# Loads that wait for earlier loads: each of the first 44 transfers into SBUF starts once another, 600 KB further ahead, has landed

## The chip, the core and the metric

The kernel runs on one NeuronCore of a Trainium2 chip. The core has a matrix engine (TensorE, PE in the tables, with its weight loads as PEld), a vector engine (DVE), a scalar engine (ACT), a general engine (POOL) and a sync engine (SP) that only issues transfers here. Each engine works through its own list of instructions in order, and semaphores hold one engine back until another, or a transfer, is done. Transfers between HBM and SBUF are carried out by 16 DMA engines. The metric is the device time of one execution in microseconds (us); lower is better.

## What is computed

Three layers follow each other, in fp32, on 4 x 576 tokens of width 512 (8 heads of 64):

```python
# 1: attention; a pooled part (means over 4 tokens) plus a local band of |i - j| < 4
out_d = sm_attn(q_d, k_d, v_d)                      # q_d, k_d, v_d: means over groups of 4
scores = np.where(mask, scale * q @ k.T, -1e9)
x = np.repeat(out_d, 4) + softmax(scores) @ v
# 2: gated feed-forward with a depthwise convolution over the tokens
h = np.maximum(x @ w_in, 0.0)                       # 512 -> 1024
x = h * sigmoid(conv3(h, conv_w)) @ w_out           # 1024 -> 512
# 3: low-rank token mixing, then a feed-forward with a residual
u = x + (x.T @ U @ V).T
out = u + np.maximum(u @ w_ch1, 0.0) @ w_ch2        # 512 -> 2048 -> 512
```

The weights of layers 2 and 3 arrive as 64-bit floats, twice the bytes of fp32, and are turned into pairs of fp32 tiles (a high and a low part) on the chip.

## The kernel before

The work is written as one long list of words, `SEQ`. Each word names a step and its indices, and the kernel emits the steps in exactly that order; every engine then executes its own share in that order. Nothing is reordered afterwards.

**Attention** runs over 16 pairs of heads, p = 0 to 15. A pair needs three loads: `lq` (`load_qk`, line 286, 576 KB), `lw` (`load_vw`, line 291, 384 KB) and `lr` (`load_vr`, line 295, 288 KB on 72 partitions). Its steps, with their lines, are: sums over groups of four (L300, DVE), scores (L317 and L324, PE), maxima, shift, exponentials and row sums (L339, L346, L352, L356), pooled scores and their exponentials (L377, L382, L389), sums of four rows of v (`vs`, L401 and L404, mostly POOL), normalisation (L370 and L394, POOL), transposes (L411 and L418, PE) and their copies out of PSUM (`c` L423, `cd` L428, ACT or DVE), the products with v (`V` L438 with 96 small matmuls, `Vd` L446, PE), and `xd` (L454) and `x` (L465), which write the result into the tile X. The step `f` (L279) is a few extra matmuls between them.

**Weights**: `wl` (`w_load`, line 485, 512 KB) loads one raw 128 x 512 tile of 64-bit words. `wd` decodes it in four steps: L495 on ACT, then L497, L499 and L502 on DVE. `wh` (L515, ACT) and `wo` (L518, mostly POOL) make the two fp32 tiles of it. 16 such tiles belong to layer 2, 32 to layer 3. In `SEQ` the loads and decodes of layer 2 stand between the steps of the attention.

**Layer 2** (g L631, acc L685) starts at about 60 us beside the attention; **layer 3** (g L759, acc L777) fills the second half of the run.

**All loads are issued by SP**, one after the other, in the order of `SEQ`: `ident` (64 KB), `maskf` (96 KB), then qk, vw, vr of pairs 0 and 1, qk and vw of pair 2, the convolution weights `craw` (24 KB), the raw tiles 1.0 to 1.2, qk of pair 3, vr of pair 2, qk of pair 4, vr of pair 3, raw tile 1.3, and so on. An issue waits for whatever still uses the buffer that it fills. Beside that there are eight semaphores for transfers, used in turn, so that a transfer also waits for the landing of the one eight before it. The 19 stores of the result come behind all the loads.

Of the kernel before, what the change touches and what calls it, by code (L numbers as in the profile page):

```python
# [9 lines left out]
U32 = mybir.dt.uint32  # L10
# [171 lines left out]
P = 128  # L182
# [5 lines left out]
def mixer_kernel(ctx, tc, consts, qk, vw_, vr_, w1, w2, cw_, u_, v_, out):  # L188
    nc = tc.nc
# [9 lines left out]
    NCH = TB // P  # L199
    XW = TB + 4  # L200
    KPB = 3
    SD = S // 4
    SCALE = D ** -0.5
    NK = cw_.shape[1] // NF
    Z = 2 if w1.dtype == U64 else 1
# [14 lines left out]
    pst = tc.alloc_tile_pool(name="pst", bufs=1, space=PSUM, side="right", reuse_waits="tile")  # L220
    pools = {}


    ident = const.tile([P, P], F32, name="ident")
    identR = pa.tile([P, P], F32R, name="identR")
    maskf = pa.tile([P, 6 * NW], F32, name="maskf")
# [4 lines left out]
    cw = const.tile([P, NK * NF], F32, name="cw")  # L231

    def load_consts():
        nc.sync.dma_start(ident, consts[:, :P])
        nc.sync.dma_start(maskf, consts[:, P:])

    def make_consts():
        nc.vector.tensor_copy(identR, ident)
# [42 lines left out]
    def slot_b(n, name):  # L281
        return (ps0 if n < 1 else pst).tile([P, 512], F32, name=name, tag=f"b{n}")

    def load_qk(p):
        t = (xu if p % 3 == 2 else pa).tile([P, 2, S], F32, name="qk", tag=("qk0", "qk1", "xu3")[p % 3])
        nc.sync.dma_start(t, qk[p])
        st[p]["qk"] = t

    def load_vw(p):
        t = st[p]["vw"] = pa.tile([P, 3, 4, D], F32, name="vw", tag="vw", bufs=3)  # L290
        nc.sync.dma_start(t.rearrange("p t a d -> p (t a d)"), vw_[p])

    def load_vr(p):
        t = st[p]["vr"] = xu.tile([72, 4, 2, 2, D], F32, name="vr", tag=f"xu{4 + p % 2}")
        nc.sync.dma_start(t.rearrange("p t h c d -> p (t h c d)"), vr_[p])

    def sums(p):
        e = st[p]
        t = e["ss"] = pa.tile([P, 2, SD], F32, name="ss", tag="ss", bufs=2)
        nc.vector.tensor_reduce(out=t.rearrange("p z x -> p (z x)"),  # L300
# [71 lines left out]
    def scores_d(p, n):  # L372
        e = st[p]
        t = slot_b(n, "Sd")
        s = e["Sd"] = t[:96, :3 * SD].rearrange("p (j x) -> p j x", j=3)
        for j in range(3):
# [7 lines left out]
    def exps_d(p):  # L384
        e = st[p]
        t = e["Pd"] = pa.tile([96, 3, SD], F32, name="Pd", tag="Pd", bufs=2)
        s = e.pop("Sd")
# [4 lines left out]
    def norm_d(p, eng):  # L392
        e = st[p]
        eng.tensor_tensor(e["Pd"], e["Pd"], e["sm"][:96, 12:].unsqueeze(2).to_broadcast([96, 3, SD]), op=ALU.mult)  # L394

# [45 lines left out]
    def pv_pooled(p):  # L441
        e = st[p]
        pt = e["PTd"].rearrange("p c (j r) -> p c j r", j=3)
        for h in range(2):
            for c in range(2):
                nc.tensor.matmul(e["O"][D * h:D * h + D, 0, 288:288 + SD].rearrange("p (j r) -> p j r", j=3),  # L446
                                 e["vd"][:, h, c], pt[:, c, :, 48 * h:48 * h + 48], start=c == 0, stop=c == 1)

    def copy_od(p, eng):
        e = st[p]  # L450
        t = e["xd"] = pa.tile([P, SD], F32, name="xd", tag="xd", bufs=2)
        src = e["O"][:, 0, 288:288 + SD]
# [21 lines left out]
    def w_home(k):  # L474
        g, i = k
        if g == 1 or NAW2 <= i < NAW2 + N1:
            return wp, f"w{i if g == 1 else i - NAW2}"
        return (pools["wa"], f"wa{i}") if i < NAW2 else (pools["wb"], f"wb{i - NAW2 - N1}")

    def w_load(*k):  # L480
        pool, tag = w_home(k)
        t = pool.tile([P, 512 * Z], U32 if Z == 2 else F32, name="raw", tag=tag)
        raws[k] = t.rearrange("p (n z) -> p n z", z=Z)
        src = (w1, w2)[k[0] - 1][k[1]]
        nc.sync.dma_start(t, src.bitcast(U32) if Z == 2 else src)

    def dec(raw, dst, step):
        if raw.shape[2] == 1:
# [31 lines left out]
    craw = const.tile([P, NK * NF * Z], U32 if Z == 2 else F32, name="craw")  # L520

    def load_conv():
        nc.sync.dma_start(craw, cw_.bitcast(U32) if Z == 2 else cw_)

    def conv_weights(step):
        dec(craw.rearrange("p (n z) -> p n z", z=Z), cw, step)
# [6 lines left out]
    def words(t, n):  # L533
        return (t[:, :n * Z].bitcast(U32) if Z == 2 else t[:, :n]).rearrange("p (n z) -> p n z", z=Z)

    def uv_load(w):
        n = u_.shape[1] if w == 0 else v_.shape[1]
        t = xu.tile([P, 1536], F32, name="uvr", tag=("xu2", "xu1")[w])
        raw = words(t, n)
        if w == 0:  # L540
            uv["t"] = t
            val = t[:, 640:640 + n]
        else:
            val = uv["t"][:, 960:960 + n]
        uv[w] = raw, val
        src = (u_, v_)[w]
        nc.sync.dma_start(raw.rearrange("p n z -> p (n z)"), src.bitcast(U32) if Z == 2 else src)

    def uv_dec(w, step):
        dec(*uv[w], step)  # L550
# [151 lines left out]
    def mix_in(g, c, odd):  # L702
        t = x2[g, c]
        pair, j = divmod(g * NCH + c, KPB * NCH)
        b = 2 * pair + odd
# [26 lines left out]
    def mix_add(pair, j):  # L732
        g, c = divmod(pair * KPB * NCH + j, NCH)
        u = U_[g][:, c]
        nc.vector.tensor_tensor(u, u, mx.pop((pair, j)), op=ALU.add)
# [44 lines left out]
    def flush4(g, c):  # L780
# [8 lines left out]
    DV, GP = nc.vector, nc.gpsimd  # L789
    ACTS = {  # L790
        "k": load_consts, "K": make_consts, "xz": x_pads, "z": clear, "sf": spin_fill, "sp": spin, "f": beat, "wm": warm,
        "lq": load_qk, "lw": load_vw, "lr": load_vr, "qs": sums, "qd": q_blocks, "S": scores, "M": maxima,
        "D": shifted, "E": exps, "R": rowsums, "re": lambda p: eps_add(p, P, 0, 15), "r": lambda p: recip(p, P, 0, 15),
        "n": lambda p: norm(p, GP), "nv": lambda p: norm(p, DV),
# [85 lines left out]
```

## Time and profile before

| | |
|---|---|
| median of 3 runs | 755.89 us (755.01 to 756.33) |
| the profiled execution, its own time | 755.43 us |
| its span, from the first to the last instruction | 753.7 us |
| PE busy, of the span | 733.5 us, 97% |
| DVE, ACT, POOL busy | 399.0, 297.2, 170.3 us |
| moved by the DMA engines | 52.43 MB |

The difference between the profiled execution's own time and its span, 1.7 us, lies around the program and is the same work for any version of it. PE is busy nearly throughout, but not evenly: the page's slices show it at 7 tenths in the first three of its 40 slices (57 us) and at 9 tenths or more from there on. So a reader should look at the first 60 us apart from the rest. Times below are counted from the start of the span.

### The profile page before, as it was taken

Reading aid. Unit: us, or ns where it says so; the run is one execution under the profiler, and the core shown is the slowest. Engines: PE = TensorE matmul, PEld = TensorE weight load, DVE = VectorE, ACT = ScalarE, POOL = GpSimd, SP = SyncE. Lnnn points to the kernel's source line nnn. Section 1 sums busy time; section 2 is a strip of 40 time slices with the busy share of each in tenths; the row PEclk is TensorE's granted clock in tenths of the full one; section 3 lists DMA queues with packets and bytes.
Section 4 is the critical chain, followed back from the end, with each engine's and each line's share of the span. In section 5 each row is a group of like instructions: output and inputs, shape, how many; then the busy total and the mean of one; then the engine's idle time right before and its main releaser. Section 6 shows DMA issues by size and latency. Waiting matters only on the chain.

```text
span 753.7 us, 15425 instructions
## 1 busy us (share of the span) xinstructions
PE 733.5 (97%) x6650; PEld 653.6 (87%) x6650; DVE 399.0 (53%) x647; ACT 297.2 (39%) x668; POOL 170.3 (23%) x161
## 2 busy tenths in 40 slices
PE   7779999999999999999999999999999999999998
PEld 5669888988988889988888989989989989898996
DVE  5798998987567984898997111311121131112112
ACT  4556777465557764766453111211111121111110
POOL 3667664352225542232222000000000000000000
PEclk9558999999999999999999999999999999999999
DMA  9855442411022001370240000100010010001001
GB/s 316 290 175 186 164 156 97 138 58 36 1 62 108 1 0 29 103 289 28 90 191 29 15 0 1 43 0 1 1 43 0 1 43 1 1 0 43 1 1 42
DMA packets 16388, 52.43 MB, mean 70 GB/s; under 512 B 1984, under 2 KB 2496, under 8 KB 16320
## 3 DMA queue, kind: packets, MB, share of 16 engines
q1 hardware_dynamic: 16320, 51.44, 19.9%
q8 instruction: 52, 0.85, 0.5%
q14 instruction: 16, 0.13, 0.1%
HBM read 46.72 MB, written 4.72 MB: 68 GB/s over the span
## 4 chain that ended last, share of the span: by engine, by line
PE 84%; DVE 9%; DMA 3%; ACT 2%; issue 2%; SPq 0%; POOL 0%; DVEq 0%; ACTq 0%
PE g L759 26%; PE acc L777 26%; PE g L631 11%; PE acc L685 10%; PE O L438 2%; DVE wval L499 2%; DMA raw<-in_w_dram 2%; DVE wval L497 1%; PE S L324 1%; DVE wval L502 1%; DMA vr<-in_vr_dram 1%; PE Sd L377 1%; PE O L446 1%; PE ut L743 1%; DVE g L658 1%
## 5 line engine op out<-in xcount | busy, mean ns | idle before, releaser
L759 PE MATMUL g<-uT,w 128*128 128x384 f32 x1152 | 214.8, 338 | 0.6 <-DVE a L768 0.6
L777 PE MATMUL acc<-w,a 128*128 128x512 f32 x864 | 208.6, 392 | 0.0
L759 PEld LDWEIGHTS g<-uT,w 128*128 128x128 f32 x1152 | 201.7, 188 | 7.5 <-DVE a L768 3.5
L768 DVE SCALAR_TENSOR_TENSOR a<-g,a 128x384 fp32r<-128x384 f32 x96 | 53.5, 557 | 264.8 <-ACT a L764 264.7
L777 PEld LDWEIGHTS acc<-w,a 128*128 128x128 f32 x864 | 160.9, 188 | 31.9 <-issue 0.6
L764 ACT ACTIVATE a<-g 128x384 fp32r<-128x384 f32 x96 | 47.1, 491 | 283.4 <-PE acc L777 165.6
L631 PE MATMUL g<-xhl,w 128*128 128x386 f32 (+1 forms) x576 | 115.4, 347 | 1.0 <-DVE ct L669 1.0
L685 PE MATMUL acc<-w,ghl 128*128 128x512 f32 x432 | 108.3, 395 | 0.0
L631 PEld LDWEIGHTS g<-xhl,w 128*128 128x128 f32 x576 | 101.8, 191 | 6.0 <-DVE ct L669 2.3
L685 PEld LDWEIGHTS acc<-w,ghl 128*128 128x128 f32 x432 | 79.6, 188 | 16.0 <-ACT u L692 0.5
L677 POOL TENSOR_TENSOR ghl<-ct,ghl 128x384 fp32r<-128x384 f32 x48 | 50.6, 1056 | 105.7 <-ACT ghl L674 86.1
L658 DVE SCALAR_TENSOR_TENSOR g<-h,cw,g 128x384 f32<-128x384 f32 x96 | 59.1, 619 | 27.2 <-ACT g L653 25.6
L518 POOL TENSOR_TENSOR w<-wval,w 128x512 fp32r<-128x512 f32 x32 | 42.8, 1341 | 58.1 <-ACT w L515 55.5
L499 DVE SCALAR_TENSOR_TENSOR wval<-raw,wval 128x512 uint32<-128x512 uint32 x48 | 43.5, 907 | 1.3
L515 ACT ACTIVATE w<-wval 128x512 fp32r<-128x512 f32 x48 | 29.8, 628 | 35.6 <-DVE wval L502 35.4
L502 DVE SCALAR_TENSOR_TENSOR wval<-raw,wval 128x512 uint32<-128x512 uint32 x48 | 41.6, 878 | 0.8
L438 PEld LDWEIGHTS O<-PT,vw 32*64 32x64 f32 x1536 | 27.9, 149 | 8.4 <-issue 7.3
L438 PE MATMUL O<-PT,vw 32*64 32x24 f32 x1536 | 29.8, 224 | 4.5 <-issue 4.4
L495 ACT ACTIVATE wval<-raw 128x512 f32<-128x512 f32 x48 | 31.3, 665 | 4.4 <-DMA raw<-in_w_dram 2.7
L637 ACT ACTIVATE h<-g 128x386 f32<-128x386 f32 (+1 forms) x48 | 23.6, 491 | 23.9 <-PE g L631 23.5
L662 ACT ACTIVATE g<-g 128x384 f32<-128x384 f32 x48 | 22.7, 473 | 21.1 <-DVE g L658 21.0
L674 ACT ACTIVATE ghl<-ct 128x384 fp32r<-128x384 f32 x48 | 25.1, 522 | 14.8 <-PE acc L685 9.8
(92 smaller groups left out, 647.3 us busy)
## 6 DMA issues: line engine op xcount, KB each, us to landing
raw<-in_w_dram SPq DMA_DIRECT2D x48, 512.0 KB
qk<-in_qk_dram SPq DMA_DIRECT2D x16, 576.0 KB
vw<-in_vw_dram SPq DMA_DIRECT2D x16, 384.0 KB
vr<-in_vr_dram SPq DMA_DIRECT2D x16, 288.0 KB
out_dram<-u SPq DMA_DIRECT2D x17, 256.0 KB
uvr<-in_v_dram SPq DMA_DIRECT2D x1, 576.0 KB
uvr<-in_u_dram SPq DMA_DIRECT2D x1, 320.0 KB
out_dram<-u SPq DMA_DIRECT2D x2, 128.0 KB
```

Of the source, the lines that this page charges most:

```text
L438: nc.tensor.matmul(o[D * h:D * h + D, jh, c:c + NQ], e["vw"][32 * s:32 * s + 32, t, a], e["PT"][32 * s:32 * s + 32, t, 32 * a:32 * a + NQ] ...
L499: nc.vector.scalar_tensor_tensor(out=d, in0=lo, scalar=29, in1=d, op0=ALU.logical_shift_right, op1=ALU.bitwise_or)
L502: nc.vector.scalar_tensor_tensor(out=d, in0=hi, scalar=0x80000000, in1=d, op0=ALU.bitwise_and, op1=ALU.bitwise_or)
L518: eng.tensor_tensor(W[k][:, 1], vals.pop(k), W[k][:, 0].bitcast(F32), op=ALU.subtract)
L631: nc.tensor.matmul(gp[n][:, :wd], w[:, a, cc], xhl[g, cc][:, b, :wd], start=cc == 0 and i == 0, stop=cc == NCC - 1 and i == 2)
L658: nc.vector.scalar_tensor_tensor(out=o, in0=inner(g, hts[n], k), scalar=cw[:, k * NF + f:k * NF + f + 1], in1=o, op0=ALU.mult, op1=ALU.add)
L677: eng.tensor_tensor(ghl[n][:, 1], cts.pop(n), ghl[n][:, 0].bitcast(F32), op=ALU.subtract)
L685: nc.tensor.matmul(acc[g][c], t[:, a, c * P:(c + 1) * P], w[:, b], start=f == 0 and i == 0, stop=f == NF - 1 and i == 2)
L759: nc.tensor.matmul(gp["3", m][:, :TB], w[:, a, cc], uT[g, cc][:, b, :TB], start=cc == 0 and i == 0, stop=cc == NCC - 1 and i == 2)
L764: nc.scalar.activation(out=t[:, 0], in_=gp["3", m][:, :TB], func=AF.Relu)
L768: nc.vector.scalar_tensor_tensor(out=t[:, 1], in0=gp.pop(("3", m))[:, :TB], scalar=0.0, in1=t[:, 0].bitcast(F32), op0=ALU.max, op1=ALU.sub ...
L777: nc.tensor.matmul(acc2[g][c], t[:, a, c * P:(c + 1) * P], w[:, b], start=f == 0 and i == 0, stop=f == NF2 - 1 and i == 2)
```

## The change

The five kinds of loads, the constants and the convolution weights go through a new function `load`, which is given the tile, the source and the size in KB. For the first 44 calls it looks back through the transfers already issued, adds up their sizes from the latest one on until the sum is 600 KB or more, and makes the new transfer wait for the landing of the one ahead of those. The order of the issues, the sizes, and all that the other engines do stay as they are.

```diff
+    WAY, NLIM = 600, 44
...
+    queue = []
+
+    def load(t, src, n):
+
+        i = nc.sync.dma_start(t, src)
+        if len(queue) < NLIM:
+            k, later = len(queue) - 1, 0
+            while k >= 0 and later < WAY:
+                later += queue[k][1]
+                k -= 1
+            if k >= 0:
+                tc.add_manual_dep(getattr(i, "ins", i), queue[k][0].name, mybir.DependencyInfo(
+                    mybir.DependencyClass.Sync, mybir.DependencyReason.DATA), reason="transfers under way")
+            queue.append((getattr(i, "ins", i), n))
...
-        nc.sync.dma_start(ident, consts[:, :P])
-        nc.sync.dma_start(maskf, consts[:, P:])
+        load(ident, consts[:, :P], 64)
+        load(maskf, consts[:, P:], 96)
...
-        nc.sync.dma_start(t, qk[p])
+        load(t, qk[p], 576)
...
-        nc.sync.dma_start(t.rearrange("p t a d -> p (t a d)"), vw_[p])
+        load(t.rearrange("p t a d -> p (t a d)"), vw_[p], 384)
...
-        nc.sync.dma_start(t.rearrange("p t h c d -> p (t h c d)"), vr_[p])
+        load(t.rearrange("p t h c d -> p (t h c d)"), vr_[p], 288)
...
-        nc.sync.dma_start(t, src.bitcast(U32) if Z == 2 else src)
+        load(t, src.bitcast(U32) if Z == 2 else src, 512)
```

No instruction moves on any engine; only the waits of SP's issues differ. On SP, at the start of the program, the kernel before has these waits from the sixth issue on (DMAHW0 to DMAHW7 are the eight semaphores of transfers: the first transfer, ident, counts on DMAHW0, maskf on DMAHW1, the first qk on DMAHW2 and so on in turn; DVE, PE and Pool stand for a buffer that the engine still uses):

```order
L286 DMA qk<-in_qk_dram 128x1152
L291 DMA vw<-in_vw_dram 128x768
L295 DMA vr<-in_vr_dram 72x1024
L286 DMA qk<-in_qk_dram 128x1152 [waits DMAHW0_49]
L291 DMA vw<-in_vw_dram 128x768 [waits DMAHW1_49]
L523 DMA craw<-in_cw_dram 128x48 [waits DMAHW2_49]
L485 DMA raw<-in_w_dram 128x1024 [waits DMAHW3_49]
L485 DMA raw<-in_w_dram 128x1024 [waits DMAHW4_49]
L485 DMA raw<-in_w_dram 128x1024 [waits DMAHW5_49]
```

The changed kernel has, at the same place on SP (line 228 is inside `load`):

```order
L228 DMA qk<-in_qk_dram 128x1152 [waits DMAHW2_49]
L228 DMA vw<-in_vw_dram 128x768 [waits DMAHW3_49]
L228 DMA vr<-in_vr_dram 72x1024 [waits DMAHW4_49]
L228 DMA qk<-in_qk_dram 128x1152 [waits DMAHW5_49]
L228 DMA vw<-in_vw_dram 128x768 [waits DMAHW6_49]
L228 DMA craw<-in_cw_dram 128x48 [waits DMAHW7_49]
L228 DMA raw<-in_w_dram 128x1024
L228 DMA raw<-in_w_dram 128x1024 [waits DMAHW0_49]
L228 DMA raw<-in_w_dram 128x1024 [waits DMAHW2_49]
```

Each issue now waits for a transfer two to four places ahead of it instead of eight. The same holds further on; at raw tile 1.3, the 19th transfer, SP's rows before are

```order
L286 DMA qk<-in_qk_dram 128x1152 [waits DMAHW6_49,DVE_49,PE_49]
L295 DMA vr<-in_vr_dram 72x1024 [waits DMAHW7_49,Pool_49]
L286 DMA qk<-in_qk_dram 128x1152 [waits DMAHW0_49,DVE_49,PE_49]
L295 DMA vr<-in_vr_dram 72x1024 [waits DMAHW1_49,DVE_49]
L485 DMA raw<-in_w_dram 128x1024 [waits DMAHW2_49]
```

and now

```order
L228 DMA qk<-in_qk_dram 128x1152 [waits DMAHW3_49,DVE_49,PE_49]
L228 DMA vr<-in_vr_dram 72x1024 [waits DMAHW4_49,Pool_49]
L228 DMA qk<-in_qk_dram 128x1152 [waits DMAHW5_49,DVE_49,PE_49]
L228 DMA vr<-in_vr_dram 72x1024 [waits DMAHW6_49,DMAHW1_49,DVE_49]
L228 DMA raw<-in_w_dram 128x1024 [waits DMAHW7_49]
```

so that raw tile 1.3 waits for the vr of pair 2 (on DMAHW7), three places ahead, instead of craw (on DMAHW2), eight ahead.

## Rows read from the trace of the kernel before

**Rows 1.** Four stretches: busy us (count) of PE, PEld, DVE, ACT, POOL; clock, DMA share, GB/s.
```profile
12.00:16.00 4.00, 2.14 (x14) 1.74 (x15) 1.71 (x2) 0.52 (x1) 2.40 (x3) 0.95 1.03 402
...
20.00:24.00 4.00, 1.96 (x77) 1.96 (x76) 2.73 (x5) 2.33 (x6) 2.92 (x3) 0.50 1.03 262
24.00:28.00 4.00, 3.56 (x62) 3.09 (x58) 3.90 (x6) 1.63 (x4) 1.57 (x1) 0.50 1.02 308
...
90.00:100.00 10.00, 10.00 (x219) 8.40 (x217) 9.89 (x14) 8.28 (x18) 6.56 (x6) 1.00 0.51 178
```

**Rows 2.** The chain that ended last, 4 to 35 us: start us, us, what.
```profile
4.16 9.37 DMA vr<-in_vr_dram
...
17.39 11.65 DMA raw<-in_w_dram
...
33.28 0.62 ACT PTd L428
33.90 0.20 ACT xd L454
...
34.12 0.77 DVE X L465
```

**Rows 3.** Timeline of PE, DVE, ACT, SP: start us, us, instruction, [idle before <-releaser].
```profile
0.74 0.38 SPq L234 DMA_DIRECT2D ident<-in_consts_dram  x1
2.57 0.23 DVE L238 CAST identR<-ident 128x128 fp32r<-128x128 f32 x1 [1.17 <-DMA ident<-in_consts_dram]
...
13.90 0.25 PE L279 MATMUL S<-mask,identR 128*128 128x192 f32 x1 [1.13 <-issue]
14.19 0.56 DVE L346 TENSOR_TENSOR P<-S,nm 128x384 f32<-128x384 f32 x1 [2.28 <-PE S L279]
...
22.04 2.54 PE L438 MATMUL O<-PT,vw 32*64 32x24 f32 x84 [2.20 <-issue]
22.49 1.35 DVE L300 TENSOR_REDUCE ss<-qk 128x288 f32<-128x1152 f32 x1 [0.95 <-DMA qk<-in_qk_dram]
...
29.12 0.67 ACT L495 ACTIVATE wval<-raw 128x512 f32<-128x512 f32 x1 [1.36 <-DMA raw<-in_w_dram]
...
29.74 1.91 PE L438 MATMUL O<-PT,vw 32*64 32x24 f32 x62 [2.18 <-issue]
29.82 0.43 DVE L497 TENSOR_SCALAR wval<-wval 128x512 uint32<-128x512 uint32 x1 [0.99 <-ACT wval L495]
...
31.58 1.24 PE L446 MATMUL O<-PTd,vd 72*64 72x144 f32 x8
```

**Rows 4.** DMA queues, a row each from 11:12, 12:19, 19:20, 20:27, 27:28.
```profile
q8 instruction: 1, 0.02, 7.5%
...
q1 hardware_dynamic: 912, 2.83, 102.3%
...
q8 instruction: 1, 0.02, 6.7%
...
q1 hardware_dynamic: 511, 1.92, 102.5%
...
q8 instruction: 1, 0.02, 6.9%
```

**Rows 5.** The page: instructions by engine, and the queue of instructions over the whole run.
```profile
PE 733.5 (97%) x6650; PEld 653.6 (87%) x6650; DVE 399.0 (53%) x647; ACT 297.2 (39%) x668; POOL 170.3 (23%) x161
...
q8 instruction: 52, 0.85, 0.5%
```

**Rows 6.** Waits from 0 to 80 us, and SP's: total us, times, longest us.
```profile
POOL vr L401 <- DMA vr<-in_vr_dram: 13.0, 5, 6.1
...
SPq L291 <- PE O L438: 71.0, 13, 10.0
```

**Rows 7.** The chain that ended last, one piece at 91 us.
```profile
91.26 1.52 PE O L438 x96
```

More of the change, by code (lines that the diff above doesn't have):

```diff
@@ L522, in load_conv @@
     def load_conv():
-        nc.sync.dma_start(craw, cw_.bitcast(U32) if Z == 2 else cw_)
+        load(craw, cw_.bitcast(U32) if Z == 2 else cw_, 24)
     def conv_weights(step):
@@ L546, in uv_load @@
         src = (u_, v_)[w]
-        nc.sync.dma_start(raw.rearrange("p n z -> p (n z)"), src.bitcast(U32) if Z == 2 else src)
+        load(raw.rearrange("p n z -> p (n z)"), src.bitcast(U32) if Z == 2 else src, 512)
     def uv_dec(w, step):
```

## The prediction, made before the changed kernel ran

> **What bounds the kernel now.** I read the busy table by stretches first, because PE's 97% over the run hides the start. In the stretches 12 to 16, 20 to 24 and 24 to 28 us PE, DVE, ACT and POOL all have idle time (DVE is busy for 1.71, 2.73 and 3.90 us of 4), while the DMA engines are full, with shares of 1.03, 1.03 and 1.02 [rows 1]. So the start waits for data. The chain of waits says the same [rows 2]: of the first 29 us it spends 9.37 us on the vr of pair 1 (issued at 4.16, landed at 13.53) and 11.65 us on raw tile 1.3 (issued at 17.39, landed at 29.04). ACT decodes that tile at 29.12, after 1.36 us of idle time; DVE, idle for 0.99 us, goes on at 29.82 [rows 3]; and the copies of ACT that stand behind it, PTd at 33.28 and xd at 33.90, release DVE's X at 34.12 [rows 2]. All later work of DVE and ACT follows in order, so I take a microsecond gained or lost at 34 us as one at the end.
>
> Beside it lies a second problem, which is the one that the change can reach directly. PE stands still three times for nothing that the profile names: 1.13 us before 13.90, 2.20 us before 22.04 and 2.18 us before 29.74, together 5.51 us [rows 3]. In each case one packet of the queue for instructions went through shortly before, in the windows 11 to 12, 19 to 20 and 27 to 28, and none in the windows between, where that queue has no row at all and the data queue fills the engines to 102% [rows 4]. That queue moved 52 packets in the run; PE has 6650 matmuls and 6650 weight loads, and 13300 / 52 is 256 instructions a packet [rows 5]. So I read these stalls as PE waiting for its own instructions, whose packet comes late because the DMA engines hold a long line of data.
>
> **How long that line is.** Before, eight transfers may be under way. When raw tile 1.3 is issued, up to seven transfers are ahead of it, and with itself they are 512 + 512 + 576 + 288 + 576 + 288 + 512 = 3264 KB, which took 11.65 us [rows 2], or 287 GB/s. After, the same tile waits for the vr of pair 2, and only qk of pair 4 and vr of pair 3 are ahead: 576 + 288 + 512 = 1376 KB. At 308 GB/s, the rate of 24 to 28 us [rows 1], that is 4.6 us from issue to landing, so the issue would move to about 24.4.
>
> **The change, part by part.**
>
> *The wait itself.* It costs SP nothing, since SP only issues. What is queued behind a waiting issue on SP are later loads; the stores come after all loads. So the cost can only be a DMA engine that runs dry. At the moment of a landing at least 600 KB are behind it, in fact 672 KB at the tightest (vw, vr or qk of the first pairs: 384 + 288 or 96 + 576) and 800 to 1088 KB for most. 672 KB at the 402 GB/s of 12 to 16 us [rows 1] last 1.71 us. A new issue needs, by the nearest row, the time of ident: issued at 0.74 with nothing ahead and first used at 2.57, 1.83 us [rows 3], of which 64 KB at 402 GB/s are 0.16, so 1.67 us. 1.71 against 1.67 is just enough, so I count 0. The upper bound: the row of ident is one transfer alone, and if the real latency were 0.1 us more, the 15 new waits up to the 19th transfer would lose 15 x 0.1, 1.5 us, of which those on the path all count. No gain is possible from this part.
>
> *The landing of raw tile 1.3.* The bytes ahead of it and their order are the same, and the engines are full either way, so the landing can only move if the packets get faster or something else gets ahead. For faster: 20 to 24 us moved 262 GB/s and 24 to 28 us 308, against 402 from 12 to 16, all at full share [rows 1]. In these stretches transfers of 72 partitions (vr) and of 128 mix in the line. If a shorter line brought the 4 x 262 + 4 x 308 = 2280 thousand bytes of these 8 us to 402 GB/s, they would take 5.7 us, a gain of 2.3; but DVE had only 0.99 us of idle time there [rows 3], and this caps it. For slower: PE's packets now come earlier, and a packet takes 0.075 of 16 engines for 1 us, 1.2 us of one engine [rows 4]; a fourth one ahead of the tile would put 1.2 us on the landing of that engine's share. Bounds: -0.99 to +1.2. I take -0.6, nearer to the gain: the three packets before 28 us are ahead of the tile in either kernel, and the slow stretch is the largest fact in the rows.
>
> *PE's stalls.* With a third of the line, the packet of instructions should come before PE runs out, and all three stalls (5.51 us) go from PE. But I credit 0 of it to the end. PE's products L446 end at 31.58 + 1.24 = 32.82 [rows 3] and ACT's xd, which reads them, comes at 33.8 only because PTd on ACT is at 33.28 [rows 2]; so PE had 0.98 us to spare at that point even with the stalls. What they would cover is the next microsecond of an earlier landing: without them PE is not late even if the tile lands 2 us sooner. The first stall also held DVE for 2.28 us up to 14.19 [rows 3], but DVE's next gate is qk of pair 3 at 22.49, where it again waits 0.95 us for the transfer [rows 3], so this time comes back as a longer wait. What is late next is the transfer in each case.
>
> The Trainium skill speaks against the premise. Its page "DMA: Bandwidth & Descriptors", section "Queues, rings and completion order", says that each engine takes turns between the queues that have work, packet by packet, so a long line on one queue should not keep another waiting. The page "Runtime: NRT & Kernel Launch", section "Instruction fetch mechanics", says that instructions come in blocks of 16 KiB and that the cost is mostly hidden. The size agrees with 0.85 MB in 52 packets [rows 5]; that the cost is hidden does not, with 5.51 us of stalls [rows 3]. If the first rule held fully, the stalls would stay as they are, and the sum would be the same, since I credit none of them; only the gaining rival below would lose its ground.
>
> *The other 25 transfers.* From about 31 us on SP waits for buffers: 71.0 us for PE's L438 alone, over 13 issues [rows 6]. The landings that the new waits ask for are then mostly in before the buffer is free, so I count 0.
>
> **Sum.** 0 - 0.6 + 0 = -0.6 us. The profiled execution took 755.43 us, 0.46 less than the median of 755.89, and the three runs lie on both sides of it. From the one the sum gives 754.8, from the other 755.3; I forecast 755.1 us.
>
> **The rivals.** What this kernel can tell from no change is about 0.2%, 1.5 us: 754.4 to 757.4 counts as the same.
>
> A, faster. The queue was the common cause, and all three idle times of DVE shrink: 2.28, 0.95 and 0.99 us, 4.22 together [rows 3]. For it speaks that both the slow packets and the late instructions stem from one long line; against it that each gate is a transfer in a line that is full before and after. If half of it is won, 2.1 us, the time is 753.2. PE's clock can add to it: it was granted 0.50, the 1.2 GHz level, from 20 to 28 us, after a stretch from 12 to 16 in which PE was busy for 2.14 us of 4 [rows 1]. At that level 84 matmuls of L438 took 2.54 us, 30 ns each [rows 3]; at 1.00, 2.4 GHz, 96 of them took 1.52 us, 16 ns each [rows 1, 7]. If a PE without stalls is back at the higher level earlier, one group of 96 on the path saves 96 x 14 ns, 1.3 us more: 751.9, say 752.0.
>
> B, slower. The waits do let the line run dry, and the data gates move out. Place: vr of pair 1 for POOL, which already waited 13.0 us for five such transfers [rows 6], qk of pair 3 for DVE, raw tile 1.3 for ACT. Price: the 1.5 us above for latency and the 1.2 us for an overtaking packet, 2.7 us together, with nothing to cover them on ACT, which stood idle before the tile anyway: 755.1 + 2.7 = 757.8. It decides from a landing of raw tile 1.3 at about 31 us on, 2 us after 29.04.
>
> C, the waits do nothing, since the eight semaphores already hold the line short enough: 755.6, between the two figures of before and the same. Against it speak the 3264 KB under way.
>
> **How the numbers follow.** Forecast and C, the same: 0.39 and 0.04. A: 0.37. B: 0.20. So faster by over 0.2% has 0.37, within 0.2% 0.43, slower by over 0.2% 0.20. The range runs from A with the clock (752.0) to just short of B's full price, 757.6: I give 0.1 to B beyond that and 0.1 to more than A with one group at the higher clock.
>
> **What would show it.** Right: PE's rows at about 13, 20 and 28 us without idle time that ends in "issue"; the packets of instructions some microseconds before 11, 19 and 27 us; raw tile 1.3 issued at 24 to 25 us, landed at 28 to 29, DVE's X at about 33.5. PE then waits for ACT's PTd instead. A shows in DVE's waits at 14.19 and 22.49 shrinking, or in an earlier rise of the clock; B in a DMA share below 0.95 between 8 and 24 us. The forecast is wrong if the tile lands after 31 us, or if PE's relief reaches DVE's X at 34 us by more than a microsecond.

## The result and the profile after

The changed kernel takes 759.82 us (median of 4 runs, 759.06 to 761.34) against 755.45 us for the kernel before on the same chip (4 runs, 754.14 to 756.33). The ratio is 1.0062, with a 95% interval from 1.0039 to 1.0084: slower by 4.4 us. The prediction said 755.1 us with a range up to 757.6, so it was wrong. The profiled execution of the changed kernel, 761.34 us with a span of 759.5, is the slowest of the four; the other three lie at 759.06 to 760.04, so its rows overstate the loss by a microsecond or two. The mean granted clock is 0.970 in both profiled executions, so the loss doesn't come from TensorE's clock.

In the changed kernel's code every line from the new function on stands 16 lower (L300 is now L316, L438 L454, L465 L481, L495 L511, L497 L513), and all loads are issued on line 228.

The table of stretches (columns as in [rows 1]) shows the start, four microseconds at a time:

```profile
12.00:16.00 4.00, 1.69 (x16) 1.41 (x12) 1.49 (x4) 1.17 (x3) 0.97 (x1) 1.00 0.83 252
20.00:24.00 4.00, 2.82 (x143) 2.67 (x132) 2.53 (x6) 3.81 (x12) 0.49 (x1) 0.50 0.89 291
24.00:28.00 4.00, 2.43 (x31) 1.83 (x26) 2.22 (x3) 1.51 (x4) 2.42 (x3) 0.50 0.89 236
```

Before, the DMA engines were full here, with shares of 1.03, 1.03 and 1.02 [rows 1]. Now the shares are 0.83, 0.89 and 0.89, and from 12 to 16 us 252 GB/s are moved in place of 402. The line of data runs dry.

Why it does is seen in the chain of waits of the first 50 us (start us, us, what). It is six transfers long up to 33.33 us, and each starts 0.01 to 0.1 us after the landing of the one above it:

```profile
1.64 4.21 DMA qk<-in_qk_dram
...
5.86 5.12 DMA qk<-in_qk_dram
...
11.01 5.08 DMA qk<-in_qk_dram
...
16.11 5.53 DMA raw<-in_w_dram
...
21.70 7.22 DMA vr<-in_vr_dram
...
28.93 4.40 DMA raw<-in_w_dram
```

In the kernel before a transfer took 9.37 or 11.65 us from issue to landing [rows 2], but up to eight of them overlapped. Now each takes 4 to 7 us and the new waits string them in a row: 4.21 + 5.12 + 5.08 + 5.53 + 7.22 + 4.40 = 31.56 of the first 33.33 us. The timeline shows what the engines get (start us, us, instruction, [idle before <-releaser]):

```profile
26.28 1.35 DVE L316 TENSOR_REDUCE ss<-qk 128x288 f32<-128x1152 f32 x1 [1.78 <-DMA qk<-in_qk_dram]
...
28.88 2.77 PE L454 MATMUL O<-PT,vw 32*64 32x24 f32 x96 [2.45 <-ACT PT L439]
...
28.93 0.33 SPq L228 DMA_DIRECT2D raw<-in_w_dram  x1
...
33.41 0.67 ACT L511 ACTIVATE wval<-raw 128x512 f32<-128x512 f32 x1 [1.83 <-DMA raw<-in_w_dram]
...
38.04 1.24 PE L462 MATMUL O<-PTd,vd 72*64 72x144 f32 x8 [3.54 <-ACT PTd L444]
38.20 0.76 DVE L481 TENSOR_TENSOR X<-O,xd 128x576 f32<-128x576 f32 x1 [1.47 <-ACT xd L470]
```

Against [rows 3]: the qk of pair 3 reaches DVE at 26.28 in place of 22.49, raw tile 1.3 reaches ACT at 33.41 in place of 29.12 (landed 33.33, before 29.04 [rows 2]), and DVE's X comes at 38.20 in place of 34.12 [rows 2], 4.08 us later. PE's three stalls that ended in "issue", 5.51 us, are gone up to 40 us; one of 0.96 us is left at 46.04. PE now waits 2.45 and 3.54 us for ACT instead.

A second, smaller loss follows at 49 us:

```profile
49.37 1.28 POOL L417 TENSOR_TENSOR vr<-vr 72x512 f32<-72x512 f32 x1 [4.09 <-DMA vr<-in_vr_dram]
49.46 2.34 DVE L513 TENSOR_SCALAR wval<-wval 128x512 uint32<-128x512 uint32 x1 [0.23 <-ACT wval L511]
51.83 1.20 DVE L515 SCALAR_TENSOR_TENSOR wval<-raw,wval 128x512 uint32<-128x512 uint32 x1
```

The sum on POOL and the first of these two DVE steps in the kernel before:

```profile
41.72 1.26 POOL L401 TENSOR_TENSOR vr<-vr 72x512 f32<-72x512 f32 x1 [0.53 <-DMA vr<-in_vr_dram]
...
45.64 1.05 DVE L497 TENSOR_SCALAR wval<-wval 128x512 uint32<-128x512 uint32 x1
```

After the change POOL waits 4.09 us for the vr in place of 0.53, its sum falls on DVE's step, and the step takes 2.34 us in place of 1.05, the one behind it 1.20 in place of 0.69; the next X is 5.61 us later than before, and that shift stays to the end (5.8 us between the two spans).

### The profile page after: what moved, and what is told of

Same layout as the page of the kernel before. It is cut to its first block, busy times and chain, and to the rows that moved or that the text cites. A ratio compares the mean times of both kernels' runs of the same rounds, so it can differ in the third digit from the quotient of the medians.

```text
span 759.5 us, 15422 instructions
## 1 busy us (share of the span) xinstructions
PE 732.4 (96%) x6650; PEld 652.7 (86%) x6650; DVE 399.4 (53%) x647; ACT 296.8 (39%) x668; POOL 169.0 (22%) x161
## 4 chain that ended last, share of the span: by engine, by line
PE 84%; DMA 7%; DVE 6%; issue 1%; ACT 1%; SPq 0%; DVEq 0%; ACTq 0%
PE g L775 26%; PE acc L793 26%; PE g L647 12%; PE acc L701 10%; DMA qk<-in_qk_dram 3%; PE O L454 3%; DMA raw<-in_w_dram 2%; DVE wval L515 1%; PE S L340 1%; PE Sd L393 1%; PE O L462 1%; DVE wval L518 1%; DMA vr<-in_vr_dram 1%; PE ut L759 1%; PE Td L434 1%
## 5 line engine op out<-in xcount | busy, mean ns | idle before, releaser
L454 PEld LDWEIGHTS O<-PT,vw 32*64 32x64 f32 x1536 | 28.0, 151 | 8.6 <-issue 3.4
L454 PE MATMUL O<-PT,vw 32*64 32x24 f32 x1536 | 29.8, 226 | 4.8 <-ACT PT L439 2.6
L511 ACT ACTIVATE wval<-raw 128x512 f32<-128x512 f32 x48 | 31.4, 668 | 6.4 <-DMA raw<-in_w_dram 4.7
L513 DVE TENSOR_SCALAR wval<-wval 128x512 uint32<-128x512 uint32 x48 | 29.3, 614 | 6.6 <-ACT wval L511 6.6
L678 ACT ACTIVATE g<-g 128x384 f32<-128x384 f32 x48 | 22.7, 473 | 21.3 <-DVE g L674 21.2
```

The costliest lines, as they stand in the source:

```text
L454: nc.tensor.matmul(o[D * h:D * h + D, jh, c:c + NQ], e["vw"][32 * s:32 * s + 32, t, a], e["PT"][32 * s:32 * s + 32, t, 32 * a:32 * a + NQ] ...
```

## The experiments

Twelve kernels were run. Each is compared with runs of the kernel before on the same chip. "The theory" below is that the added waits let the line of data run dry; the rivals stand with each run.

### How far the limit reaches, and which waits cost

Limit of 1200 KB:

```diff
-    WAY, NLIM = 600, 44
+    WAY, NLIM = 1200, 44
```

> The limit is 1200 KB in place of 600, nothing else. Dry line (the DMA engines run out of work while SP waits for the last of the 16 to finish a transfer): more is queued at each landing, so the share from 4 to 28 us rises from 0.80-0.89 to 0.95 or more, raw tile 1.3 lands at 29 to 31 us (33.33 in the changed kernel, 29.04 before), and the time is 755.5 to 757.5, at least 2 us under the changed kernel. If the loss is not the line's (contention of DVE, ACT and POOL, or PE's clock), the landing may come back but the time stays at 759 to 760. PE's stalls that end in 'issue' come back in part, 1 to 4 us of the 5.51.

Limit of 2000 KB:

```diff
-    WAY, NLIM = 600, 44
+    WAY, NLIM = 2000, 44
```

> The limit is 2000 KB. Dry line: hardly any wait is left that finds the line short, share 1.0, raw tile 1.3 lands at 29.0 to 29.5, time 755 to 756.3 as the kernel before; PE's stalls are near 5 us. If a shorter line were a gain of its own (packets of instructions in time, engines still full), this or the run with 1200 KB would be below 754.4.

Waits on the first 19 transfers only:

```diff
-    WAY, NLIM = 600, 44
+    WAY, NLIM = 600, 19
```

> 600 KB, but only the first 19 transfers wait (to raw tile 1.3); the other 25 are as before. If the start carries the loss: raw tile 1.3 lands at 33 us as in the changed kernel, X follows at 38, and the time is 758.5 to 760. If the later waits carry it (X of the changed kernel is 4.1 us late at 38 us, but 5.6 from 46 us on): 757.5 to 758.5, 1.5 us under the changed kernel, with the vr that POOL waits for at 49 us landing 1.5 us earlier in relation to X.

Waits from the 20th transfer on only:

```diff
-            if k >= 0:
+            if k >= 0 and len(queue) >= 19:
```

> 600 KB, but only the 20th to the 44th transfer wait. If the start carries the loss: the time is 755 to 756.3, raw tile 1.3 lands at 29.0 and PE's three stalls of 5.51 us are back. If the later waits have a price of their own: 757 or more, with the shift between 40 and 55 us.

Limit of 300 KB:

```diff
-    WAY, NLIM = 600, 44
+    WAY, NLIM = 300, 44
```

> The limit is 300 KB, 44 transfers. Dry line: the loss goes on growing; raw tile 1.3 lands at 38 to 44 us, DVE's X at 43 to 49, time 766 to 776. Rival (the loss is a fixed cost of waiting at all, or of contention): 759 to 762, as with 600.

| kernel | median us | before beside it | ratio, 95% interval | raw tile 1.3 at ACT | X |
|---|---|---|---|---|---|
| 300 KB (two runs) | 765.33 | 755.65 | 1.0124, 1.0096 to 1.0153 | 35.79 | 41.02 |
| 600 KB (the change) | 759.82 | 755.45 | 1.0062, 1.0039 to 1.0084 | 33.41 | 38.20 |
| 600 KB, first 19 | 758.95 | 755.61 | 1.0048, 1.0036 to 1.0060 | 32.20 | 36.53 |
| 600 KB, from the 20th | 756.74 | 755.61 | 1.0020, 1.0004 to 1.0035 | 30.00 | 35.41 |
| 1200 KB | 756.78 | 755.61 | 1.0014, 0.9999 to 1.0029 | 28.36 | 33.71 |
| 2000 KB | 755.84 | 755.61 | 1.0006, 0.9994 to 1.0019 | 28.39 | 33.78 |

The dose decides: 9.7, 4.4, 1.2 and 0.2 us for 300, 600, 1200 and 2000 KB. That excludes a fixed price of waiting. The run with 300 KB came 0.7 us under its expected 766, and its tile and X 2 us sooner than the 38 and 43 us expected. The two halves of the change add up within their intervals: 3.3 us for the first 19 transfers (2.7 to 4.5 by the ratio) and 1.1 for the others (0.3 to 2.6) make the 4.4 of both. With the first 19 alone X stood at 36.53, a little earlier than the 38 expected; two kernels with the same first 19 waits differ by 1.2 us in raw tile 1.3 (33.41 and 32.20 at ACT). With the waits from the 20th on, X comes 1.29 us later than before, though the transfers up to raw tile 1.3 wait there as they did before. So single profiles scatter by more than a microsecond, and smaller differences of X between two of them show nothing.

The price of the later waits has a place. With the waits from the 20th on alone, the second loss of the changed kernel is there, and the engines run dry before it (the stretch from 24 to 28 us):

```profile
24.00:28.00 4.00, 4.00 (x82) 3.58 (x76) 3.93 (x5) 1.12 (x3) 2.15 (x2) 0.50 0.72 174
...
47.50 1.43 POOL L417 TENSOR_TENSOR vr<-vr 72x512 f32<-72x512 f32 x1 [5.02 <-DMA vr<-in_vr_dram]
47.84 2.50 DVE L518 SCALAR_TENSOR_TENSOR wval<-raw,wval 128x512 uint32<-128x512 uint32 x1
```

POOL waits 5.02 us for the vr, and a DVE step that took 1.27 us before (at 44.45) takes 2.50. X is 1.28 us late ahead of this place and 2.21 behind it. With the waits on the first 19 alone POOL doesn't wait for this vr, and X is 2.41 us late both before and behind.

With 1200 KB the share from 8 to 16 us was 0.96 to 0.97 and the tile came sooner than in the kernel before, yet no time was gained; the next group takes that up.

The run with 2000 KB shows what two of PE's stalls are worth. Its rows of PE beside DVE's X:

```profile
24.77 2.77 PE L454 MATMUL O<-PT,vw 32*64 32x24 f32 x96 [0.71 <-ACT PT L439]
27.46 1.24 PE L462 MATMUL O<-PTd,vd 72*64 72x144 f32 x8
28.63 1.76 PE L393 MATMUL Sd<-ss,qd 128*96 128x144 f32 x6
33.61 1.23 PE L462 MATMUL O<-PTd,vd 72*64 72x144 f32 x8 [3.23 <-ACT PTd L444]
```

Two of the three stalls are gone (2.20 and 2.18 us before [rows 3]; 0.17 us and none here; the first, 1.13 before, is 1.53), and PE is done with the first L462 at 28.70 in place of 32.82 [rows 3], 4.1 us sooner. X comes at 33.78, 0.34 us sooner. What PE won, it waits away again: 3.23 us for ACT's PTd. The stalls were expected to stay, near 5 us. Nor do they follow the limit: with 1200 KB, the shorter line, they came to 4.21 us, with 2000 KB to 1.70. Why they go in one run and not in another is open.

### The price of a wait by itself

The first 19 loads of the kernel without any computation, in six phases:

```diff
+        phase("free", 1 << 30, False)
+        phase("six", 600, False)
+        phase("twelve", 1200, False)
+        phase("three", 300, False)
+        phase("evenfree", 1 << 30, True)
+        phase("evensix", 600, True)
```

> Only the first 19 loads, in the kernel's order and sizes (7.6 MB), and 19 one-column copies on DVE that mark their landings; all of the computation is left out and the result is filled with zeros. Six phases, twice, each begun when the one before has landed: no limit (but the eight semaphores), 600 KB, 1200 KB, 300 KB, then no limit and 600 KB with the vr loads spread over 128 partitions. Dry line: 20 to 23 us from the first issue to the last landing without a limit, 2.5 to 5 us more with 600, under 1 more with 1200, 8 or more with 300; this with no engine at work and few packets of instructions. If the last of the 16 engines is late because vr fills only a part of them, the even phases differ by less than 1.5 us between no limit and 600. Rival (the loss needs the engines' work or the packets of instructions beside it): all phases without a limit, with 1200 and with 600 within 1 us.

The timeline of its first turn: the first issue, and for each phase the DVE operation that closes it (the next phase starts 0.19 us later):

```profile
0.73 0.38 SPq L42 DMA_DIRECT2D identfree<-in_consts_dram  x1
...
26.12 0.16 DVE L77 TENSOR_TENSOR mfree<-identfree,mfree 128x1 f32<-128x1 f32 x1
...
57.48 0.16 DVE L77 TENSOR_TENSOR msix<-identsix,msix 128x1 f32<-128x1 f32 x1
...
85.64 0.16 DVE L77 TENSOR_TENSOR mtwelve<-identtwelve,mtwelve 128x1 f32<-128x1 f32 x1
...
121.31 0.16 DVE L77 TENSOR_TENSOR mthree<-identthree,mthree 128x1 f32<-128x1 f32 x1
...
144.13 0.16 DVE L77 TENSOR_TENSOR mevenfree<-identevenfree,mevenfree 128x1 f32<-128x1 f32 x1
...
172.99 0.16 DVE L77 TENSOR_TENSOR mevensix<-identevensix,mevensix 128x1 f32<-128x1 f32 x1
```

Counted from one of these operations to the next, the phases last 25.4, 31.4, 28.2, 35.7, 22.8 and 28.9 us; in the second turn 28.4, 30.5, 28.7, 34.6, 22.3 and 28.1. On the mean, 600 KB cost 30.9 - 26.9 = 4.0 us, 1200 KB 1.5 and 300 KB 8.2, with no computation beside the loads. The phase without a limit scatters by 3 us and was expected at 20 to 23, so the 4.0 are rough (6.0 in the first turn, 2.1 in the second), but the order of the limits is the same in both turns. A loss of the size of the kernel's (3.3 us for the first 19 transfers in the timed runs) thus needs neither the engines' work nor their instructions: the rival falls. Over the 15 new waits 4.0 us are 0.27 us each. One guess of mine fell with it: that a wait costs because vr fills only a part of the 16 engines. With as many bytes on 128 partitions in place of vr, 600 KB still cost 28.5 - 22.6 = 5.9 us (6.1 and 5.8 in the two turns).

One size only, 12 transfers of 576 KB, by how much is queued behind the landing that an issue waits for:

```diff
+        phase("none", 0)
+        phase("one", 576)
+        phase("two", 1152)
+        phase("three", 1728)
+        phase("free", 1 << 30)
```

> Loads alone: 12 transfers of 576 KB (qk), with one-column copies on DVE that mark the landings; the whole computation is left out and the result is filled with zeros. Five phases, twice: an issue waits for the landing of the last transfer (0 KB behind the landing), of the one ahead (576 KB behind it), two ahead (1152), three ahead (1728), and no wait but that of the eight semaphores. From the issue to the landing of a transfer of 288 KB with nothing left of the line, 2.99 us were read, and 3.4 to 5.2 for 576 KB. So with 0 behind 3.5 to 4.2 us a transfer. If an issue needed 1.67 us until its data flows and no more (the prediction's step): 1.4 to 1.5 us a transfer from 576 KB on (576 KB last 1.43 us at 402 GB/s, a little under 1.67, so a loss of some 0.2) and no loss at 1152. If the line is dry for longer than that, because an issue takes over 2 us and the last of the 16 engines is what is waited for: 2.0 to 2.6 us a transfer with 576 behind, 1.6 to 1.8 with 1152, and within 0.1 of no wait only with 1728.

Its first turn, in the same way:

```profile
0.73 39.43 SPq L37 DMA_DIRECT2D qknone<-in_qk_dram  x12
...
43.68 0.16 DVE L54 TENSOR_TENSOR mnone<-qknone,mnone 128x1 f32<-128x1 f32 x1
...
72.43 0.16 DVE L54 TENSOR_TENSOR mone<-qkone,mone 128x1 f32<-128x1 f32 x1
...
95.14 0.16 DVE L54 TENSOR_TENSOR mtwo<-qktwo,mtwo 128x1 f32<-128x1 f32 x1
...
115.55 0.16 DVE L54 TENSOR_TENSOR mthree<-qkthree,mthree 128x1 f32<-128x1 f32 x1
...
128.52 0.15 DVE L53 COPY mfree<-qkfree 128x1 f32<-128x1 f32 x1 [1.22 <-DMA qkfree<-in_qk_dram]
129.91 0.15 DVE L53 COPY mfree<-qkfree 128x1 f32<-128x1 f32 x1 [1.23 <-DMA qkfree<-in_qk_dram]
...
135.60 0.16 DVE L54 TENSOR_TENSOR mfree<-qkfree,mfree 128x1 f32<-128x1 f32 x1
```

| KB behind the landing | phase, us (two turns) | over the free phase | waits | lost per wait |
|---|---|---|---|---|
| 0 | 43.0, 43.5 | 23.1 | 11 | 2.10 |
| 576 | 28.8, 28.6 | 8.6 | 10 | 0.86 |
| 1152 | 22.7, 23.0 | 2.8 | 9 | 0.31 |
| 1728 | 20.4, 20.5 | 0.3 | 8 | 0.04 |
| no wait but the eight semaphores | 20.1, 20.2 | | | |

A transfer of 576 KB lands every 1.38 us in a full line (the marks from 128.52 to 129.91, and on to 132.66, three transfers in 4.14 us), 427 GB/s. With nothing behind the landing, 2.10 us are lost at each issue. This holds the start of the new transfer and the report of the landing together; the rows don't split it. With 576 KB behind, 2.10 - 1.38 = 0.72 us should be lost, and 0.86 were. With 1152 KB the line lasts 2.77 us, which should be enough, and still 0.31 us are lost. What makes up that remainder is open. One candidate, not shown, is that an issue waits for the last of the 16 engines while others are already ahead; no row here tells the engines apart.

The Trainium skill, page "DMA: Bandwidth & Descriptors", section "Anatomy of one DMA — SWDGE (gpsimd) path", gives a transfer a fixed part of about 2.0 us and a variable one of bytes over 436 thousand per us, for another issuing engine. This run agrees, with 2.10 us and 427 GB/s on SP's queue.

### What an earlier landing is worth

The order of two loads changed, without any added wait (raw tile 1.2 behind the qk of pair 3, the qk of pair 4 behind raw tile 1.3):

```diff
-       "... wl.1.1 qs.0 wl.1.2 S.0.2 ... M.0 lq.3 D.0 ... qd.1 lq.4 M.1 ... wd.1.0.1 wl.1.3 "
+       "... wl.1.1 qs.0 S.0.2 ... M.0 lq.3 wl.1.2 D.0 ... qd.1 M.1 ... wd.1.0.1 wl.1.3 lq.4 "
```

> The kernel before, without any wait added, but two loads later in the order: raw tile 1.2 behind qk of pair 3, and qk of pair 4 behind raw tile 1.3. The bytes ahead of the two gates fall by 512 and 576 KB. If the landings of qk of pair 3 and of raw tile 1.3 set DVE's X, and PE's stalls cost nothing: qk of pair 3 lands 1.0 to 1.5 us sooner than 22.47, raw tile 1.3 1.0 to 2.0 sooner than 29.04, X comes at 32.3 to 33.4 in place of 34.12, and the time falls by 0.7 to 1.8 us although PE's stalls of some 5 us stay. If PE's stalls held the start: X stays at 34.1 and the time at 755.6.

Median 755.49 us, ratio 0.9994 (0.9981 to 1.0007): the same. The loads came far sooner than expected. DVE no longer waits for the qk of pair 3, and ACT takes raw tile 1.3 at 28.28 without waiting for its landing. X came at 33.65, only 0.47 us sooner. The table of stretches of this run says why for the time from 20 us on:

```profile
20.00:24.00 4.00, 3.77 (x91) 3.69 (x91) 3.64 (x7) 3.37 (x10) 2.90 (x4) 0.53 1.03 282
24.00:28.00 4.00, 2.48 (x62) 2.02 (x64) 3.92 (x4) 0.78 (x3) 3.10 (x3) 0.50 1.02 406
28.00:32.00 4.00, 4.00 (x60) 3.26 (x56) 3.88 (x5) 1.57 (x3) 1.39 (x1) 0.50 0.97 377
```

DVE is busy for 3.64, 3.92 and 3.88 us of 4: with the data early, DVE's own work is the bound there. But it starts on that work late, because of PE:

```profile
14.93 0.25 PE L279 MATMUL S<-mask,identR 128*128 128x192 f32 x1 [1.52 <-issue]
15.21 0.56 DVE L346 TENSOR_TENSOR P<-S,nm 128x384 f32<-128x384 f32 x1 [2.67 <-PE S L279]
```

The first of PE's three stalls is still there, 1.52 us, and DVE stands idle for 2.67 us behind it; from 15.21 on it waits only 0.25 us more until 32 us. With 2000 KB it is the same (1.53 and 2.67 us). So once the loads are early, this stall lies on the way to X, and the time is the one that was expected if PE's stalls held the start (755.6). No run is without this stall and has the qk of pair 3 early, so what it is worth is not shown.

DVE's steps also stretch where POOL works beside them, three of them here:

```profile
24.34 1.64 DVE L499 SCALAR_TENSOR_TENSOR wval<-raw,wval 128x512 uint32<-128x512 uint32 x1
26.01 1.64 DVE L502 SCALAR_TENSOR_TENSOR wval<-raw,wval 128x512 uint32<-128x512 uint32 x1
...
28.02 0.69 DVE L499 SCALAR_TENSOR_TENSOR wval<-raw,wval 128x512 uint32<-128x512 uint32 x1
28.75 1.64 DVE L502 SCALAR_TENSOR_TENSOR wval<-raw,wval 128x512 uint32<-128x512 uint32 x1
```

1.64 us in place of 0.69 for the same form. The kernel before had two such steps and 0.99 us of idle time [rows 3]; here there is a third step and no idle time. The 0.99 us were thus not there to be won.

All kernels with the computation, by DVE's sums of the qk of pair 3, raw tile 1.3 at ACT, the time that DVE waited for that tile behind the sums, and X (the lower rows belong to runs that follow):

| kernel | sums of qk, pair 3 | raw tile 1.3 at ACT | DVE's wait for it | X | X after the sums |
|---|---|---|---|---|---|
| before | 22.49 | 29.12 | 0.99 | 34.12 | 11.63 |
| 300 KB | 29.42 | 35.79 | none | 41.02 | 11.60 |
| 600 KB | 26.28 | 33.41 | 1.46 | 38.20 | 11.92 |
| 600 KB, first 19 | 24.67 | 32.20 | 2.24 | 36.53 | 11.86 |
| 600 KB, from the 20th | 23.79 | 30.00 | none | 35.41 | 11.62 |
| 1200 KB | 22.77 | 28.36 | none | 33.71 | 10.94 |
| 2000 KB | 22.17 | 28.39 | none | 33.78 | 11.61 |
| changed order | 22.01 | 28.28 | none | 33.65 | 11.64 |
| 1200 KB, first 19 | 22.52 | 29.35 | 1.21 | 34.41 | 11.89 |
| vr in two pieces | 22.84 | 29.65 | 1.18 | 34.74 | 11.90 |
| two pieces, changed order | 22.80 | 30.55 | none | 35.92 | 13.12 |
| 80 partitions | 22.57 | 28.67 | none | 34.19 | 11.62 |

From 22.01 to 29.42 the start of these sums moves by 7.4 us, and in ten of the twelve X keeps 11.6 to 11.9 us behind it. It also keeps 4.3 to 5.5 us behind raw tile 1.3, because both landings move together, so the table doesn't tell which of the two sets X. In five runs DVE still waited for the tile behind the sums, so there the tile was the later gate; fewer stretched steps then made up for the wait. To be early gained 0.5 us of X at most, which is within the scatter. To be late costs its full amount: with 300 KB the sums start 6.93 us later than before and X comes 6.90 us later.

The limit of 1200 KB on the first 19 transfers alone, to find where the run with 1200 KB lost its 0.4 us of X:

```diff
-    WAY, NLIM = 600, 44
+    WAY, NLIM = 1200, 19
```

> 1200 KB, and only the first 19 transfers wait. The run with 1200 KB and 44 transfers had X 0.41 us earlier, and lost 0.9 us from 43 us on, where a DVE operation took 2.76 us in place of 0.62 beside POOL's sum of a vr that landed 0.96 us later, and 0.5 us at 64. If those were the late waits' doing: X at 33.6 to 33.9, no such operation at 43 us, time 755.0 to 755.6. If the collision is the earlier X's doing: 756 to 757, as with all 44.

Median 756.54 us, ratio 1.0010 (0.9997 to 1.0023); X at 34.41. This run doesn't decide: the data itself came a microsecond later than with 1200 KB and 44 waits (raw tile 1.3 at 29.35 in place of 28.36) under the same waits on these 19 transfers, so the earlier X that it was to protect wasn't there. The DVE step at 44.07 took 0.62 us, as before. An earlier X isn't needed for a stretched step: the run with waits from the 20th on has one (2.50 us) with a later X.

Three tries for a version that beats both kernels, since loads spread evenly were 4.3 us faster alone (22.6 against 26.9 us). First the vr loads in two pieces of 2 KB a partition:

```diff
-        nc.sync.dma_start(t.rearrange("p t h c d -> p (t h c d)"), vr_[p])
+        nc.sync.dma_start(t.rearrange("p (a t) h c d -> p a (t h c d)", a=2), vr_[p].rearrange("a p n -> p a n"))
```

> The kernel before, without any added wait; each vr load is written as two pieces of 2 KB for each of its 72 partitions in place of one of 4 KB (the array lies accordingly in HBM). If the pieces spread the load over more of the 16 engines, as the even phases of the run with loads alone suggest (22.2 us in place of 26.6), qk of pair 3 lands 0.5 to 1.5 us sooner than 22.47 and raw tile 1.3 1 to 3 us sooner than 29.04. If DVE's own work bounds the start once the data is 0.5 us sooner (X came at 33.65 to 33.78 in the runs with 1200 KB, 2000 KB and the changed order, wherever raw tile 1.3 landed between 25 and 28.4): X at 33.4 to 33.8, time 754.6 to 755.6. If the data bounds it throughout: X at 32 to 33, time under 754.5.

Then the two pieces together with the changed order:

```diff
-       "... qs.0 wl.1.2 S.0.2 ... lq.3 D.0 ... lq.4 M.1 ... wl.1.3 "
+       "... qs.0 S.0.2 ... lq.3 wl.1.2 D.0 ... M.1 ... wl.1.3 lq.4 "
...
-        nc.sync.dma_start(t.rearrange("p t h c d -> p (t h c d)"), vr_[p])
+        nc.sync.dma_start(t.rearrange("p (a t) h c d -> p a (t h c d)", a=2), vr_[p].rearrange("a p n -> p a n"))
```

> The vr loads in two pieces and the changed order (raw tile 1.2 behind qk of pair 3, qk of pair 4 behind raw tile 1.3) together. If DVE bounds the start: X again at 33.4 to 33.8, time 754.4 to 755.4, no more than either alone. If the data bounds it: X at 31 to 32.8, time under 754.

Then 80 partitions in place of 72:

```diff
-        t = st[p]["vr"] = xu.tile([72, 4, 2, 2, D], F32, name="vr", tag=f"xu{4 + p % 2}")
+        t = xu.tile([80, 4, 2, 2, D], F32, name="vr", tag=f"xu{4 + p % 2}")
+        st[p]["vr"] = t[:72]
```

> The kernel before, without any added wait; each vr load brings 80 partitions in place of 72 (eight rows of zeros, 320 KB in place of 288). The Trainium skill, page DMA: Bandwidth & Descriptors, section on why a DMA increments its semaphore by 16, says that a transfer uses as many of the 16 engines as divide its count of rows: 12 for 72, 16 for 80. The rest goes without it: with the load spread as in the even phases of the run with loads alone (22.6 us in place of 26.9), qk of pair 3 lands 0.5 to 1.5 us sooner than 22.47 and raw tile 1.3 1.5 to 3 us sooner than 29.04. If DVE's own work bounds the start once the data is half a microsecond sooner: X at 33.4 to 33.8, time 754.6 to 755.6. If the data bounds it throughout: X at 32 to 33, time under 754.4.

None is faster: ratios 1.0002 (0.9989 to 1.0014), 1.0000 (0.9988 to 1.0013) and 1.0006 (0.9994 to 1.0018), with X at 34.74, 35.92 and 34.19. The pieces didn't bring the data sooner (sums of the qk of pair 3 at 22.84 in place of 22.49). With the changed order added, raw tile 1.2 became the late one: ACT waited 1.94 us for it at 24.55, and X came 1.80 us later. With 80 partitions raw tile 1.3 reached ACT at 28.67, 0.45 us sooner, but the sums stood at 22.57. From 20 to 24 us the engines were again full at 257 GB/s (262 before [rows 1]). Why the full line is that slow there no run explains; the loads alone moved 327 and 297 GB/s in the two phases without a limit, and 376 with vr spread.

## Why the prediction was wrong, point by point

**The step that failed is "The wait itself", counted at 0 with an upper bound of 1.5 us.** It set 672 KB of queued data, 1.71 us, against 1.67 us that a new issue needs, and took just enough for enough. The need was sized from the one row of ident, 1.83 us less its data; measured by itself it is 2.10 us. And the 1.71 us, at the 402 GB/s of one stretch, are 672 / 576 x 1.38 = 1.61 us at the measured 1.38 us for 576 KB. So each of the tightest waits is short by about half a microsecond, not by nothing. Only three of the 15 new waits are that tight; five have 864 KB behind them, 2.07 us, and are short by 0.03. By this sum the step should have had 3 x 0.49 + 5 x 0.03 = 1.6 us, and the loads alone lost 4.0 on the mean, and 5.9 with vr spread. As far as these figures go, the rest is lost at waits with enough behind them, as the 0.31 us at 1152 KB are: the step took a wait to be free once the data behind it lasts as long as the need, and that didn't hold either, for a reason that stays open. The bound of 0.1 us per wait was five times too small there and, at 0.27 us on the mean, nearly three times over the 15 waits. The rows held a warning: a price that is compared with a nearly equal one has a sign only if both are known to a few hundredths of a microsecond. The Trainium skill's page "DMA: Bandwidth & Descriptors", section "Anatomy of one DMA — SWDGE (gpsimd) path", speaks against the step as well: an estimate from its two figures, given for another issuing engine, is 2.0 - 1.58 = 0.4 us lost at a wait with 672 KB behind it. The measured 0.86 us at 576 KB and 0.31 at 1152 put it higher, at about 0.8 (an estimate between the two).

**"The engines are full either way", in the step on raw tile 1.3, fell with it.** The share went to 0.80 to 0.89 from 8 us on, and the tile landed at 33.33 in place of 29.04, outside the bounds of -0.99 to +1.2. It took 4.40 us from its issue, near the 4.6 that were forecast for the shorter line, but the issue came at 28.93 in place of 24.4. The step also took one gate for the only one. The chain of waits [rows 2] passes through raw tile 1.3, but with 300 KB, 2000 KB and the changed order DVE didn't wait for that tile, and X kept its distance from the sums of the qk of pair 3. A chain names what ended last in one execution; it doesn't say how far behind the next gate is.

**The faster packets, -0.6, did not come from a shorter line.** In the changed kernel 291 and 236 GB/s were moved in the two stretches from 20 to 28 us, at a share of 0.89; that is 264 on the mean, against 285 before [rows 1]. With 2000 KB the landing did come 0.7 us sooner (ACT 28.39 against 29.12), and X 0.34 us sooner; that is within the scatter of single profiles.

**PE's stalls, credited with 0: right for two of them, not shown for the first.** All three went, as forecast, and nothing of their 5.51 us reached the end: PE waits for ACT in their place, and in the run with 2000 KB, without the second and the third, a PE that is 4.1 us ahead leaves X where it was to 0.34 us. The first held DVE for 2.28 us, and the step expected that time to come back as a wait for the qk of pair 3. In the changed order that qk was early, and the stall stood on the way to X. The rows say less on why the stalls went. The packets of instructions came in the windows 9 to 10, 19 to 20 and 25 to 26 us, two of them some 2 us sooner, but PE is itself later at the places where it ran out before, and over the runs the stalls don't follow the limit.

**The other 25 transfers, credited with 0, cost 1.1 us** (ratio 1.0020, 1.0004 to 1.0035). The step argued that SP waits for buffers there anyway. In the run with these waits alone the share from 24 to 28 us was 0.72 with 174 GB/s, against 1.02 and 308 before [rows 1]: the line ran dry there too. It is not true, then, that the awaited landings are mostly in before the buffers are free; the 20th transfer, issued at 19.31 before, waited for a landing until 27.72. The step had also read its row too widely: the 71.0 us over 13 issues [rows 6] are those of the whole run. Up to 90 us, SP's row in the kernel before is

```profile
SPq L291 <- PE O L438: 23.6, 6, 5.7
```

**Rival B had the mechanism, its place and its signs**: a share below 0.95 between 8 and 24 us (0.80 from 8 to 12, and 0.83 and 0.89 above), a tile after 31 us, gates that move out on DVE, ACT and POOL. It had a chance of 0.20 and a price of 2.7 us; the price measured 4.4. Rival A had the largest chance after the forecast, 0.37. Of its three idle times of DVE the first shrank, from 2.28 us to 1.01 before 13.94, and came back right behind it as a wait of 1.61 us for the qk of pair 2 at 16.11; the other two grew, from 0.95 to 1.78 us and from 0.99 to 1.46. The first one's rows in the changed kernel:

```profile
13.94 0.56 DVE L362 TENSOR_TENSOR P<-S,nm 128x384 f32<-128x384 f32 x1 [1.01 <-PE S L295]
16.11 1.35 DVE L316 TENSOR_REDUCE ss<-qk 128x288 f32<-128x1152 f32 x1 [1.61 <-DMA qk<-in_qk_dram]
```

## What to carry to other kernels

A limit on loads under way is free only if what is queued behind the awaited landing outlasts the start of a new transfer with room to spare: the start took 2.10 us here, and 576 KB (1.38 us) lost 0.86 us per wait, 1152 KB (2.77 us) 0.31 and 1728 KB nothing to speak of. Measure both sides with loads alone before comparing them, since a difference of 0.04 us has no sign. Before crediting an earlier landing, move it both ways and see whether the engine behind it follows: here it followed when late and hardly at all when early. Where it doesn't follow, look for what holds it next: in two runs here one of PE's stalls stood there.

## What the runs showed of the hardware

A transfer of 576 KB issued with nothing under way lands after 3.5 us, of which 1.38 are its data at 427 GB/s; the rest, about 2.1 us, is lost each time the line is empty. Even 1152 KB behind a landing, 2.77 us of data, didn't hide it wholly.

DVE's steps on two inputs (128 x 512) take 0.69 us alone and mostly 1.64 (2.50 once above) where they start while POOL is at work; a step that had started first kept its 0.69 (at 28.02 in the changed order, POOL from 28.45). A one-input step of 0.42 us took 2.59 and 2.34 beside POOL in the changed kernel. So the time between two gates of DVE is not fixed: idle time that the changed order removed came back as a longer step.

The 19 loads alone took 26.9 us with vr on its 72 partitions, and 22.6 with as many bytes on 128 partitions in place of vr (they come from another array, in shorter rows, so the count of partitions is not the only difference). The Trainium skill, page "DMA: Bandwidth & Descriptors", section "Why a DMA increments its semaphore by 16 and not by 1", puts a transfer on the largest number of engines up to 16 that divides its count of rows, by which 72 rows use 12 (an estimate). The times point the same way, but no row here tells the engines apart, and with 80 rows the whole kernel won nothing.
